# Leaving out or narrowing the third block of an expert's tokens, and packing the rest of the gating into fewer steps

## The chip, the cores and the metric

The kernel runs on one core of one Trainium2 chip. The metric is the device time of one execution in microseconds (us). Before the change the median of three runs is 567.98 us (566.25 to 568.43). The profile shows one further execution.

## The reference

Three layers follow each other. Their inputs are 4 batches of 576 positions with 8 heads of 64; the output of the first layer is read as 2304 tokens of 512 values.

```
attn = softmax(q k^T / 8 + bias(s), causal) v          # layer 1, x = [2304, 512]
expert = argmax(x @ w_gate)                            # layer 2: top-1 of 8 experts
x[t] = gate_w[t] * (relu(x[t] @ w1[e]) @ w2[e])        #   for the tokens t of expert e
logits = x @ phi                                       # layer 3: soft mixture, 32 slots
slot_in = softmax(logits, over tokens).T @ x
slot_out = relu(slot_in @ w1'[e]) @ w2'[e]             #   4 slots for each of 8 experts
out = softmax(logits, over slots) @ slot_out
```

## The kernel before

**Stages.** Attention runs from the start to about 215 us, the gating of the last batch to about 235 us, the eight experts of layer 2 from 239.6 to 503 us, and the slot experts and the output follow. An untaken branch (`overflow`, for experts with more tokens than planned) lies at 235 to 239 us.

**An expert.** The experts are sorted by their number of tokens. Place `e` has room for `WIDTH[e]` token columns, 352, 336, 320, 304, 304, 288, 256 and 256, at most CAP = 384, which is three blocks of 128. An expert is 16 steps in the order `STEPS`: eight h steps (12 matmuls into `h`, L1004, the hidden layer) and eight y steps (12 matmuls into `y`, L1004). A weight chunk is split for each step into a high part (`whi`, a cast on ACT, L893) and a low part (`wlo`, a subtraction on DVE, L895), two steps ahead, in three buffers. `hhi` (ACT, L1028) and `hlo` (DVE, L1029) are the same split of h.

**Gathering.** `gather(e)` (L911) fetches the tokens of an expert with three indirect DMAs that POOL issues, one for each block of 128, into `xg`; `xt_unit` (L998) turns them with 12 PE transposes into `xT`. The transposes for expert e+1 stand before the last two steps of expert e.

**The rest of the gating.** For the first expert's successors the gating is not finished when the first expert starts. `late_units` holds 13 pieces: `sort_a` (the sort of the experts, DVE), `g3`, five `gt` (`la` and `cbo`, L734 and L737, four on DVE and one on POOL), `sort_regs` (ACT and SP read the order into registers), `g4` (the PE matmuls `tb`, L745, and `idxu`, L746), `sort_b` (the gather's indices `sidxu`, L577 to L580), `pads` (L1215 to L1222), `close_att` (memory of the attention is given to the weight ring) and `gather(1)`. `merge` lays these evenly between the first expert's steps 1 to 13. Each engine runs its instructions in the order in which the program issues them.

**The post stage.** `post_units(e)` is merged between the steps of expert e+1; that of the last expert has no steps around it. `pl`: logits `lgp` (L1064), four products of 32 output rows each and 384 columns, one for each 128 values of a token, each in its own 32 columns of the PE array. `p1`: `ltp` (L1083), the logits by token, the running maximum over tokens. `py(t)`: `yTp` (L1073), the block's tokens turned back. `p2`, `p3`: the maximum `mt`, `mr`, `mb`, then the exponentials `Lm` and `al`. `p4`: `si` (L1116), for each block a product of 32 rows and 512 columns, and on DVE `SI = SI * ac + si` (L1120), a running sum of 96 rows, 32 for each block. `pc`, `pc2`: the softmax over slots `L`, which POOL scatters with one indirect DMA for each block into `c_d` (L1146). After the last post stage `sps` (L1262) reads all 96 rows of `SI`, and the slot experts (`hp`, `acc`) begin. In the last post stage PE runs matmuls on constants (`warm`, L245) after the pieces that the table `WARM` names by their place in the list.

Of the kernel before, what the change touches and what calls it, by code (L numbers as in the profile page):

```python
# [71 lines left out]
def kernel(ctx, tc, qk, vm, vt, s, wg, w1, w2, phi, m1, m2, m3, out, dbg=None):  # L72
# [830 lines left out]
            refill(i)  # L903

    def gather(e, idx, ov=False, early=False):
        for t in range(3):
            g = ytok[:, t, :] if ov else wpool[0].tile([128, DM], F32, tag="xg", name=f"xg{e}_{t}", bufs=3)
            if early:
                nc.gpsimd.memset(g, 0.0)
            rows = N - S if early else N + 1  # L910
            nc.gpsimd.indirect_dma_start(  # L911
                out=g, out_offset=None, in_=xg_d[0:rows],
                in_offset=bass.IndirectOffsetOnAxis(ap=idx[:, t:t + 1], axis=0),
                bounds_check=rows - 1, oob_is_err=False)
            xg_t[e, t] = g
# [70 lines left out]
    pmk = mp.tile([128, E, 3], F32, name="pmk")  # L986
    idxm = mp.tile([128, E, 3], U32, name="idxm")

    def xt_copy(k, tp):
        nc.scalar.copy(xT[:, 0, k, :], tp[:, 0:CAP])  # L990
        nc.vector.tensor_tensor(out=xT[:, 1, k, :], in0=tp[:, 0:CAP], in1=xT[:, 0, k, :].bitcast(F32),
                                op=ALU.subtract)

    def xt_unit(e, k):
        def f():
            tp = ps.tile([128, 512], F32, tag="tp", name=f"xTp{e}_{k}", bufs=2)
            for t in range(3):
                nc.tensor.transpose(tp[:, 128 * t:128 * t + 128], xg_t[e, t][:, 128 * k:128 * k + 128], ident)  # L998
            xt_copy(k, tp)
        return f  # L1000

    def product(w_, terms):
# [52 lines left out]

    def post_units(e, pad, idx, final=False):
        d = {}

        def pl():
            lg = ps.tile([128, CAP], F32, tag="tp", name=f"lgp{e}", bufs=2)
            for k in range(4):
                nc.tensor.matmul(lg[32 * k:32 * k + 32, :], lhsT=phi_sb[:, k, :], rhs=yT[:, k, :], start=True, stop=True,  # L1064
                                 skip_group_check=True)
            d["l4"] = ytok[:, 2, 0:CAP]
            (halves if final else nc.scalar.copy)(d["l4"], lg)

        def py(t):
            def f():  # L1070
                tp = ps.tile([128, 512], F32, tag=f"y{t}" if final else "tp", name=f"yTp{e}_{t}", bufs=1 if final else 2)
                for k in range(4):
                    nc.tensor.transpose(tp[:, 128 * k:128 * k + 128], yT[:, k, 128 * t:128 * t + 128], ident)  # L1073
                if t == 1 and not final:
                    nc.vector.tensor_copy(ytok[:, t, :], tp)
                else:
                    nc.scalar.copy(ytok[:, t, :], tp)
# [34 lines left out]
        def p4():
            al, Lm = d["al"], d["Lm"]
            si = ps.tile([128, DM], F32, tag="tp", name=f"si{e}", bufs=2)
            for t in range(3):
                nc.tensor.matmul(si[32 * t:32 * t + 32, :], lhsT=Lm[:, t, :], rhs=ytok[:, t, :], start=True, stop=True)  # L1116
            ac = mp.tile([128, 32], F32, tag="ac", name=f"ac{e}", bufs=1)
            nc.vector.transpose(ac, al)
            for x in (slice(0, 256), slice(256, 512)) if final else (slice(0, 512),):
                nc.vector.scalar_tensor_tensor(out=SI[:, x], in0=SI[:, x], scalar=ac[0:96, 0:1], in1=si[0:96, x],  # L1120
                                               op0=ALU.mult, op1=ALU.add)

        def p4b():
            al, Lm = d["al"], d["Lm"]
            nc.vector.tensor_tensor(out=esum, in0=esum, in1=al, op=ALU.mult)
            es = mp.tile([128, 32], F32, tag="es", name=f"es{e}", bufs=1)
            nc.vector.tensor_reduce(out=es, in_=Lm.rearrange("p t s -> p s t"), axis=AX.X, op=ALU.add)
            nc.vector.tensor_tensor(out=esum, in0=esum, in1=es, op=ALU.add)

        def pc():  # L1130
            L = mp.tile([128, 3, 32], F32, tag="L", name=f"L{e}", bufs=2)
            mx = mp.tile([128, 3], F32, tag="cmx", name=f"cmx{e}", bufs=1)
            nc.vector.tensor_reduce(out=mx, in_=d["Lm"], axis=AX.X, op=ALU.max)
            nc.vector.tensor_tensor(out=L, in0=d["Lm"], in1=mx.unsqueeze(2).to_broadcast([128, 3, 32]), op=ALU.subtract)
            nc.scalar.activation(out=L, in_=L, func=ACTF.Exp)
            d["L"] = L

        def pc2():
            L = d["L"]
            sm = mp.tile([128, 3], F32, tag="csm", name=f"csm{e}", bufs=1)  # L1140
# [3 lines left out]
            nc.vector.tensor_tensor(out=L, in0=L, in1=sm.unsqueeze(2).to_broadcast([128, 3, 32]), op=ALU.mult)  # L1144
# [12 lines left out]
    def overflow(over):  # L1157
        with tc.If(over > 0, label="over"):  # L1158
# [20 lines left out]
            for e in range(E):  # L1179
# [8 lines left out]
                with tc.For_i(0, times, 1):  # L1188
# [289 lines left out]
```

## Time and profile before

| what | value |
|---|---|
| median of three runs | 567.98 us |
| the profiled execution | 566.11 us |
| its span, first to last instruction | 564.4 us |
| PE busy | 537.0 us, 95% |
| DVE, ACT, POOL busy | 368.6, 300.6, 175.9 us |
| mean granted TensorE clock | 0.990 of full speed |
| on the chain that ended last | PE 52%, of it h and y of the experts 36% |

Times in the rows below are microseconds from the start of the span. Busy time is the share in which an engine has an instruction in flight; PE's matmuls overlap, so the time that a group of them costs is read from the distance of the starts, which the chain of waits gives as the group's piece.

### The profile page before, as it was taken

The numbers are of one execution on the slowest core, as the hardware profiler recorded it, in microseconds if no ns is written. First come the engines' busy times: TensorE is split into PE (matmuls) and PEld (weight loads), VectorE is DVE, ScalarE is ACT, GpSimd is POOL, SyncE is SP. The second block draws the span as 40 slices with busy tenths as digits, with TensorE's granted clock in tenths as the row PEclk, the third lists the DMA queues.
The fourth block names the chain that finished last, engine by engine and source line by source line (L and its number), as shares of the span: only waits on it lengthen the run. The fifth ranks groups of instructions, "written<-read, shape, count | busy, mean of one in ns | idle before, by whom it ended". The sixth has DMA issues, their size and how long they took to land.

```text
span 564.4 us, 11552 instructions
## 1 busy us (share of the span) xinstructions
PE 537.0 (95%) x4148; PEld 429.3 (76%) x4152; DVE 368.6 (65%) x1023; ACT 300.6 (53%) x782; POOL 175.9 (31%) x208
## 2 busy tenths in 40 slices
PE   8688899999999999899699999999999999999994
PEld 3466666766776666699699999999999898973464
DVE  6687779779887954476356666566766767653253
ACT  5477777687687765143343545445455555541122
POOL 6543236632843706012202204032220403025300
PEclk9899999999999999999899999999999999999998
DMA  4765662766487131201468768687874644479996
GB/s 120 247 227 150 203 220 82 210 224 202 127 249 230 48 129 63 92 2 28 175 214 302 279 237 293 244 327 281 296 273 162 201 158 153 150 253 339 396 351 186
DMA packets 40787, 114.60 MB, mean 203 GB/s; under 512 B 5775, under 2 KB 14289, under 8 KB 38800
## 3 DMA queue, kind: packets, MB, share of 16 engines
q1 hardware_dynamic: 27040, 68.81, 37.2%
q10 hardware_dynamic: 10560, 37.77, 18.8%
q0 software_dynamic: 3120, 7.19, 3.7%
q8 instruction: 35, 0.57, 0.4%
q14 instruction: 32, 0.26, 0.1%
HBM read 98.52 MB, written 11.16 MB: 194 GB/s over the span
## 4 chain that ended last, share of the span: by engine, by line
PE 52%; issue 3%; DMA 1%; DVE 0%; POOL 0%; ACT 0%; POOLq 0%
PE y L1004 18%; PE h L1004 18%; PE acc L1366 3%; PE hp L1327 3%; PE yTp L1073 2%; PE xTp L998 2%; PE si L1116 1%; PE op L1397 1%; PE lgp L1064 1%; DMA xg<-xg_d,sidxu 1%; PE ltp L1083 1%; PE cTp L1311 0%; PE mb L1102 0%; PE hTp L1343 0%; PE warm L245 0%
## 5 line engine op out<-in xcount | busy, mean ns | idle before, releaser
L1004 PE MATMUL h<-xT,whi 128*128 128x304 f32 (+5 forms) x512 | 110.4, 306 | 2.1 <-PEq L1158 2.1
L895 DVE TENSOR_TENSOR wlo<-chunk,whi 128x512 fp32r<-128x512 f32 x125 | 85.5, 688 | 31.7 <-ACT whi L893 31.0
L893 ACT CAST whi<-chunk 128x512 fp32r<-128x512 f32 x128 | 78.9, 620 | 27.4 <-PE y L1004 23.9
L1004 PEld LDWEIGHTS h<-xT,whi 128*128 128x128 f32 x512 | 83.0, 188 | 3.2 <-issue 2.6
L1004 PE MATMUL y<-hhi,whi 128*128 128x256 f32 (+5 forms) x256 | 81.5, 318 | 0.0
L1146 POOL DMA_INDIRECT c_d<-L,idxm x24 | 31.5, 1311 | 156.9 <-DVE L L1144 141.0
L491 ACT COPY aT<-tp 128x512 f32<-128x512 f32 (+3 forms) x128 | 55.5, 452 | 43.1 <-PE tp L484 31.3
L1004 PE MATMUL y<-hlo,whi 128*128 128x256 f32 (+5 forms) x256 | 77.4, 302 | 0.0
L1004 PE MATMUL y<-hhi,wlo 128*128 128x256 f32 (+5 forms) x256 | 77.3, 302 | 0.0
L1004 PE MATMUL h<-xT,wlo 128*128 128x256 f32 (+5 forms) x256 | 77.0, 301 | 0.0
L425 DVE CUSTOM_DVE_ANT_0 sa<-sc,mask 128x384 f32<-128x384 f32 (+3 forms) x128 | 60.5, 484 | 20.2 <-PE sc L422 17.9
L435 ACT ACTIVATE sa<-sa,mx 128x128 f32<-128x128 f32 (+3 forms) x128 | 71.2, 561 | 1.1 <-DVE mx L425 0.8
L1028 ACT ACTIVATE hhi<-h 128x304 fp32r<-128x304 f32 (+5 forms) x64 | 27.1, 423 | 68.1 <-PE h L1004 67.1
L538 PE MATMUL oTp<-aT,v 128*64 128x320 f32 (+4 forms) x448 | 59.4, 374 | 0.0
L1029 DVE SCALAR_TENSOR_TENSOR hlo<-h,hhi 128x304 fp32r<-128x304 f32 (+5 forms) x64 | 30.2, 472 | 42.6 <-ACT hhi L1028 42.2
L484 PE MATMUL tp<-ident,sa 128*128 128x128 f32 x320 | 53.4, 284 | 3.4 <-ACT sa L435 3.2
L1004 PEld LDWEIGHTS y<-hhi,whi 128*128 128x128 f32 x256 | 48.7, 190 | 10.4 <-issue 5.9
L422 PE MATMUL sc<-ks,qs 128*128 128x384 f32 (+3 forms) x128 | 50.1, 394 | 2.4 <-DVE mx L425 1.4
L484 PEld LDWEIGHTS tp<-ident,sa 128*128 128x128 f32 x320 | 35.0, 142 | 21.9 <-issue 11.2
L387 POOL TENSOR_TENSOR ks<-qk,ks 64x576 fp32r<-64x576 f32 x31 | 45.5, 1481 | 15.1 <-ACT ks L367 11.1
L1004 PEld LDWEIGHTS y<-hlo,whi 128*128 128x128 f32 x256 | 48.8, 191 | 0.0
L1004 PEld LDWEIGHTS y<-hhi,wlo 128*128 128x128 f32 x256 | 48.6, 190 | 0.0
(288 smaller groups left out, 958.1 us busy)
## 6 DMA issues: line engine op xcount, KB each, us to landing
chunk<-in_w_dram ACTq DMA_DIRECT2D x56, 512.0 KB, 5.5
chunk<-in_m_dram SPq DMA_DIRECT2D x45, 512.0 KB, 5.6
qk<-in_qk_dram SPq DMA_DIRECT2D x15, 1152.0 KB, 5.7
chunk<-in_m_dram ACTq DMA_DIRECT2D x16, 512.0 KB, 5.2
kb<-ks SPq DMA_DIRECT2D x15, 288.0 KB, 3.6
v<-in_vm_dram SPq DMA_DIRECT2D x16, 256.0 KB, 5.7
chunk<-in_w_dram SPq DMA_DIRECT2D x8, 512.0 KB, 6.5
xg_d<-xr SPq DMA_DIRECT2D x16, 256.0 KB, 3.6
```

The source lines that it names most:

```text
L387: eng.tensor_tensor(out=ks, in0=qk_t[p][64:128, 1, hh], in1=ks.bitcast(F32), op=ALU.subtract)
L422: nc.tensor.matmul(sc[:, :ext], lhsT=qs_t[p % 2][:, j, hh, 64 * hh + 128 * st:64 * hh + 128 * st + 128], rhs=ks[:, hh, :ext], start=(j == ...
L425: nc.vector.tensor_tensor_reduce(out=sa[:, o:o + ext], in0=sc[:, :ext], in1=mask[:, 512 - ext:512], scale=1.0, scalar=3.0e38, op0=ALU.add, ...
L435: nc.scalar.activation(out=x, in_=x, func=ACTF.Exp, bias=mx[:, st:st + 1], scale=-1.0, accum_out=rsum[:, b, st, 2 * k + hh:2 * k + hh + 1])
L484: nc.tensor.transpose(tp[:, 128 * c:128 * c + 128], src(hh, st, jt), ident)
L491: nc.scalar.copy(o, i)
L538: nc.tensor.matmul(o[c][64 * hh:64 * hh + 64, lo - 256 * c:hi - 256 * c], lhsT=v_t[p][:n, jt, hh, :], rhs=aT[:n, hh, jt, lo:hi], start=(jt ...
L893: nc.scalar.copy(hi, raw)
L895: eng.tensor_tensor(out=lo, in0=raw, in1=hi.bitcast(F32), op=ALU.subtract)
L1004: nc.tensor.matmul(out[:, :w_], lhsT=a, rhs=b[:, :w_], start=first, stop=last, skip_group_check=True)
L1029: nc.vector.scalar_tensor_tensor(out=lo[:, :w_], in0=h[:, :w_], scalar=0.0, in1=hi[:, :w_].bitcast(F32), op0=ALU.max, op1=ALU.subtract)
L1146: nc.gpsimd.indirect_dma_start(out=c_d[t], out_offset=bass.IndirectOffsetOnAxis(ap=idx[:, t:t + 1], axis=0), in_=L[:, t, :], in_offset=Non ...
```

## The change

Four things change.

1. `post_units` and `xt_unit` work on the columns that the expert has. With `w_ = WIDTH[e]` and `nt` blocks (three for places 0 to 5, two for places 6 and 7), `lgp` has `w_` columns for 384, and the third block's transposes, products, softmax columns, gather and scatter are left out for places 6 and 7.
2. For these two places the rows 64 to 95 of `SI` still have to be scaled: POOL does it with a new instruction, `SI[g:96] * ac`, in `p4`. DVE's `SI` keeps the first 64 rows.
3. The 13 late units are merged with the first expert's steps 1 to 8; steps 9 to 13 follow without any.
4. `py(2)` is no piece of the list for the last two places. `WARM` is unchanged, so its places 6 and 9 now mean `p3` (it was `pc`) and nothing (it was `p4`).

```
     def gather(e, idx, ov=False, early=False):
-        for t in range(3):
+        for t in range(3 if ov or early else -(-WIDTH[e] // 128)):
...
-            for t in range(3):
+            for t in range(-(-w // 128)):
                 nc.tensor.transpose(tp[:, 128 * t:128 * t + 128], xg_t[e, t][:, 128 * k:128 * k + 128], ident)
-            xt_copy(k, tp)
+            xt_copy(k, tp, w)
...
+        w_ = CAP if ov else WIDTH[e]
+        nt = -(-w_ // 128)
...
-                nc.tensor.matmul(lg[32 * k:32 * k + 32, :], lhsT=phi_sb[:, k, :], rhs=yT[:, k, :], start=True, stop=True,
+                nc.tensor.matmul(lg[32 * k:32 * k + 32, 0:w_], lhsT=phi_sb[:, k, :], rhs=yT[:, k, 0:w_], start=True, stop=True,
...
-            for t in range(3):
+            for t in range(nt):
                 nc.tensor.matmul(l[:, t, :], lhsT=d["l4"][:, 128 * t:128 * t + 128], rhs=repI, start=True, stop=True,
...
         def p4():
             al, Lm = d["al"], d["Lm"]
-            si = ps.tile([128, DM], F32, tag="tp", name=f"si{e}", bufs=2)
-            for t in range(3):
-                nc.tensor.matmul(si[32 * t:32 * t + 32, :], lhsT=Lm[:, t, :], rhs=ytok[:, t, :], start=True, stop=True)
             ac = mp.tile([128, 32], F32, tag="ac", name=f"ac{e}", bufs=1)
             nc.vector.transpose(ac, al)
+            si = ps.tile([128, DM], F32, tag="tp", name=f"si{e}", bufs=2)
+            for t in range(nt):
+                r = min(128, w_ - 128 * t)
+                nc.tensor.matmul(si[32 * t:32 * t + 32, :], lhsT=Lm[:r, t, :], rhs=ytok[:r, t, :], start=True, stop=True)
+            g = 32 * nt
+            if nt < 3:
+                nc.gpsimd.tensor_scalar(out=SI[g:96], in0=SI[g:96], scalar1=ac[g:96, 0:1], scalar2=None, op0=ALU.mult)
             for x in (slice(0, 256), slice(256, 512)) if final else (slice(0, 512),):
-                nc.vector.scalar_tensor_tensor(out=SI[:, x], in0=SI[:, x], scalar=ac[0:96, 0:1], in1=si[0:96, x],
+                nc.vector.scalar_tensor_tensor(out=SI[0:g, x], in0=SI[0:g, x], scalar=ac[0:g, 0:1], in1=si[0:g, x],
                                                op0=ALU.mult, op1=ALU.add)
...
-            for t in range(3):
+            for t in range(nt):
                 nc.gpsimd.indirect_dma_start(
                     out=c_d[t], out_offset=bass.IndirectOffsetOnAxis(ap=idx[:, t:t + 1], axis=0),
                     in_=L[:, t, :], in_offset=None, bounds_check=N - 1, oob_is_err=False)
+        third = [py(2)] if nt > 2 else []
         if final:
-            return [pl, p1, py(0), py(1), p2, py(2), pc, p3, pc2, p4, p4b]
-        return [pl, p1, py(0), p2, pc, py(1), p3, pc2, py(2), p4, p4b]
+            return [pl, p1, py(0), py(1), p2, *third, pc, p3, pc2, p4, p4b]
+        return [pl, p1, py(0), p2, pc, py(1), p3, pc2, *third, p4, p4b]
...
-            for u in merge(steps[1:14], (post if e else late_units + [lambda: gather(1, eidx(1))])):
+            k = 14 if e else 9
+            for u in merge(steps[1:k], (post if e else late_units + [lambda: gather(1, eidx(1))])) + steps[k:14]:
```

The places where this moves instructions, in the order in which each engine has them:

DVE, in the first expert, before: from the last `la` to the gather's indices `sidxu` (`hlo_5` belongs to the sixth h step).

```order
L734 TENSOR_SCALAR la_4_7345<-io_125,lane_7141 64x128
L737 TENSOR_SCALAR cbo_4_7347<-io_128,ch_7139,tid 64x144
L895 TENSOR_TENSOR wlo_7350<-chunk_2858,whi_7349 128x512
L1029 SCALAR_TENSOR_TENSOR hlo_5_7366<-h_7087,hhi_5_7365 128x352
L746 TENSOR_TENSOR idxu<-idxf,tb_7369 128x144
L895 TENSOR_TENSOR wlo_7377<-chunk_2044,whi_7376 128x512
L577 CAST tidx<-idxu 128x24
```

The same on DVE now (`hlo_3` belongs to the fourth h step):

```order
L1031 SCALAR_TENSOR_TENSOR hlo_3_7290<-h_7096,hhi_3_7289 128x352
L734 TENSOR_SCALAR la_4_7293<-io_125,lane_7121 64x128
L737 TENSOR_SCALAR cbo_4_7295<-io_128,ch_7119,tid 64x144
L746 TENSOR_TENSOR idxu<-idxf,tb_7297 128x144
L895 TENSOR_TENSOR wlo_7305<-chunk_1357,whi_7304 128x512
L577 CAST tidx<-idxu 128x24
```

The indices stood behind the sixth h step's `hlo_5` and stand now behind the fourth's `hlo_3`; between `cbo_4` and `idxu` there was a whole step, and now there is nothing.

POOL, at the end of the last expert's post stage, before: its three scatters and what follows (names in brackets are semaphores; DMASW are those of POOL's own DMAs).

```order
L1146 DMA c_d_62<-L_10576,idxm 2304x32 [waits DMASW5_49,DMASW0_49,DVE_49]
L1146 DMA c_d_63<-L_10576,idxm 2304x32 [waits DMASW6_49,DMASW1_49]
L1146 DMA c_d_64<-L_10576,idxm 2304x32 [waits DMASW7_49]
L1284 MEMSET hz_10646 128x1024 [waits DMAHW3_49,PE_49,DMAHW6_49,Activation_49,Pool_49]
L1290 DMA c_10648<-c_d_62 128x192 [waits DMAHW4_49,DMASW0_49,DMAHW7_49,PE_49,Activation_49]
```

The same on POOL now:

```order
L1157 DMA c_d_62<-L_10543,idxm 2304x32 [waits DVE_49,Pool_49]
L1157 DMA c_d_63<-L_10543,idxm 2304x32
L1129 TENSOR_SCALAR SI<-SI,ac_10570 32x512 [waits DMASW6_49,DMASW5_49,DVE_49]
L1297 MEMSET hz_10607 128x1024 [waits DMAHW3_49,PE_49,DMAHW6_49,Activation_49,Pool_49]
L1303 DMA c_10609<-c_d_62 128x192 [waits DMAHW4_49,DMAHW7_49,PE_49,Activation_49]
```

Two scatters are left, and the new multiplication of `SI` stands behind them; it waits for the semaphores that these two scatters raise when they land (the first raises DMASW5, the second DMASW6).

PE, at the same place, before: from the maximum to the first product of `sps`.

```order
L1094 MATMUL mt_10563<-ident,m_10547 1x128 [waits DVE_49]
L245 MATMUL warm_10568<-const-bfloat16-1.0 128x512 [waits PE_49]
L1073 MATMUL yTp_2_10570<-ident,yy 128x128 x4
L245 MATMUL warm_10581<-const-bfloat16-1.0 128x512 [waits PE_49]
L1102 MATMUL mb_10584<-mr_10565,ones 128x32 [waits DVE_49]
L1116 MATMUL si_10606<-yy,Lm_10544 32x512 [waits Activation_49]
L245 MATMUL warm_10614<-const-bfloat16-1.0 128x512 [waits PE_49]
L1262 MATMUL sps_10618<-repI,SI 128x32 [waits DVE_49]
```

The same on PE now:

```order
L1101 MATMUL mt_10536<-ident,m_10520 1x128 [waits DVE_49]
L245 MATMUL warm_10541<-const-bfloat16-1.0 128x512 [waits PE_49]
L1109 MATMUL mb_10548<-mr_10538,ones 128x32 [waits DVE_49]
L245 MATMUL warm_10556<-const-bfloat16-1.0 128x512 [waits PE_49]
L1126 MATMUL si_10572<-yy,Lm_10517 32x512 [waits Activation_49]
L1275 MATMUL sps_10579<-repI,SI 128x32 [waits DVE_49,Pool_49]
```

`mb` no longer stands behind the third block's transposes and a pair of `warm` matmuls, no `warm` stands between `si` and `sps` any more, and `sps` waits for POOL as well as for DVE.

## Rows read from the trace of the kernel before

**Rows 1.** Windows: length, busy (count) PE, PEld, DVE, ACT, POOL, PEclk, DMA share, GB/s

```profile
270.00:280.00 10.00, 7.08 (x37) 6.88 (x38) 3.61 (x7) 3.82 (x9) 1.71 (x2) 0.83 0.29 106
280.00:500.00 220.00, 220.00 (x1635) 205.45 (x1634) 146.48 (x343) 112.32 (x243) 47.44 (x38) 1.00 0.68 236
```

**Rows 2.** Waits of PE, 200 to 300 us: total, times, longest

```profile
PE xTp L998 <- DMA xg<-xg_d,sidxu: 4.4, 2, 2.4
```

**Rows 3.** Chain of waits around the second expert: start, length, what

```profile
266.86 6.35 DMA xg<-xg_d,sidxu
...
273.25 1.11 PE xTp L998 x4
274.37 2.92 PE y L1004 x12
...
277.94 1.94 PE y L1004 x12
...
283.55 0.78 PE lgp L1064 x8
...
286.37 0.59 PE ltp L1083 x6
...
288.88 0.44 PE yTp L1073 x4
```

**Rows 4.** The same chain, 285 to 455 us

```profile
305.60 0.99 PE si L1116 x6
```

**Rows 5.** Instructions of PE in order: start, length, what

```profile
258.91 1.58 PE L745 MATMUL tb<-cbo,la 128*128 128x144 f32 x10
```

**Rows 6.** Instructions of DVE in the first expert, in order

```profile
251.89 0.53 DVE L1029 SCALAR_TENSOR_TENSOR hlo<-h,hhi 128x352 fp32r<-128x352 f32 x1 [0.44 <-ACT hhi L1028]
...
256.87 0.27 DVE L734 TENSOR_SCALAR la<-io,lane 64x128 f32<-64x128 f32 x1
257.06 0.34 DVE L737 TENSOR_SCALAR cbo<-io,ch,tid 64x144 f32<-64x144 f32 x1
...
260.53 0.30 DVE L746 TENSOR_TENSOR idxu<-idxf,tb 128x144 uint32<-128x144 f32 x1 [0.40 <-PE tb L745]
...
263.15 0.18 DVE L580 CAST sidxu<-sidx 128x24 uint32<-128x24 f32 x1
```

**Rows 7.** Instructions of POOL in the first expert, in order

```profile
264.13 1.11 POOL L911 DMA_INDIRECT xg<-xg_d,sidxu  x1 [13.57 <-issue]
```

**Rows 8.** Instructions of all engines, end of the last post stage

```profile
507.58 0.28 DVE L1096 TENSOR_REDUCE mr<-mt 1x32 f32<-1x128 f32 x1 [0.37 <-PE mt L1094]
507.70 0.60 PE L1073 MATMUL yTp<-ident,yy 128*128 128x128 f32 x4
...
508.67 0.40 PE L1102 MATMUL mb<-mr,ones 1*128 1x32 f32 x2
...
510.29 0.26 DVE L1144 TENSOR_TENSOR L<-L,csm 128x96 f32<-128x96 f32 x1
...
510.82 0.98 POOL L1146 DMA_INDIRECT c_d<-L,idxm  x1 [11.04 <-DVE ac L1118]
...
511.38 1.09 PE L1262 MATMUL sps<-repI,SI 96*128 96x32 f32 x8
...
512.11 0.98 POOL L1146 DMA_INDIRECT c_d<-L,idxm  x1 [0.30 <-PE sps L1262]
```

**Rows 9.** DMAs issued from 495 to 520 us: what, queue, count, median us to landing

```profile
c_d<-L,idxm POOLq DMA_INDIRECT x6, 4.1
```

**Rows 10.** Line L1146, all 24 scatters of the run

```profile
DMA to landing us min/median/max: 3.2/4.7/6.6
```

**Rows 11.** Groups of POOL: out<-in, shape, count, busy us, mean ns

```profile
L737 POOL TENSOR_SCALAR cbo<-io,ch,tid 128x144 f32<-128x144 f32 x13 | 12.6, 968 | 0.0
L734 POOL TENSOR_SCALAR la<-io,lane 128x128 f32<-128x128 f32 x13 | 8.3, 640 | 22.6 <-DVE lane L711 22.4
...
L895 POOL TENSOR_TENSOR wlo<-chunk,whi 128x512 fp32r<-128x512 f32 x3 | 3.7, 1266 | 0.0
```

More of the change, by code (lines that the diff above doesn't have):

```diff
@@ L987, with xt_copy, xt_unit @@
     idxm = mp.tile([128, E, 3], U32, name="idxm")
-    def xt_copy(k, tp):
-        nc.scalar.copy(xT[:, 0, k, :], tp[:, 0:CAP])
-        nc.vector.tensor_tensor(out=xT[:, 1, k, :], in0=tp[:, 0:CAP], in1=xT[:, 0, k, :].bitcast(F32),
+    def xt_copy(k, tp, w):
+        nc.scalar.copy(xT[:, 0, k, 0:w], tp[:, 0:w])
+        nc.vector.tensor_tensor(out=xT[:, 1, k, 0:w], in0=tp[:, 0:w], in1=xT[:, 0, k, 0:w].bitcast(F32),
                                 op=ALU.subtract)
-    def xt_unit(e, k):
+    def xt_unit(e, k, ov=False):
+        w = CAP if ov else WIDTH[e]
         def f():
             tp = ps.tile([128, 512], F32, tag="tp", name=f"xTp{e}_{k}", bufs=2)
-            for t in range(3):
+            for t in range(-(-w // 128)):
                 nc.tensor.transpose(tp[:, 128 * t:128 * t + 128], xg_t[e, t][:, 128 * k:128 * k + 128], ident)
-            xt_copy(k, tp)
+            xt_copy(k, tp, w)
         return f
@@ L1054, in step_unit, with post_units @@
         return f
-    def post_units(e, pad, idx, final=False):
+    def post_units(e, pad, idx, final=False, ov=False):
         d = {}
+        w_ = CAP if ov else WIDTH[e]
+        nt = -(-w_ // 128)
         def pl():
@@ L1063, in pl @@
             for k in range(4):
-                nc.tensor.matmul(lg[32 * k:32 * k + 32, :], lhsT=phi_sb[:, k, :], rhs=yT[:, k, :], start=True, stop=True,
+                nc.tensor.matmul(lg[32 * k:32 * k + 32, 0:w_], lhsT=phi_sb[:, k, :], rhs=yT[:, k, 0:w_], start=True, stop=True,
                                  skip_group_check=True)
             d["l4"] = ytok[:, 2, 0:CAP]
-            (halves if final else nc.scalar.copy)(d["l4"], lg)
+            (halves if final else nc.scalar.copy)(d["l4"][:, 0:w_], lg[:, 0:w_])
         def py(t):
@@ L1071, in f @@
                 tp = ps.tile([128, 512], F32, tag=f"y{t}" if final else "tp", name=f"yTp{e}_{t}", bufs=1 if final else 2)
+                r = min(128, w_ - 128 * t)
                 for k in range(4):
-                    nc.tensor.transpose(tp[:, 128 * k:128 * k + 128], yT[:, k, 128 * t:128 * t + 128], ident)
+                    nc.tensor.transpose(tp[:r, 128 * k:128 * k + 128], yT[:, k, 128 * t:128 * t + r], ident)
                 if t == 1 and not final:
-                    nc.vector.tensor_copy(ytok[:, t, :], tp)
+                    nc.vector.tensor_copy(ytok[:r, t, :], tp[:r])
                 else:
-                    nc.scalar.copy(ytok[:, t, :], tp)
+                    nc.scalar.copy(ytok[:r, t, :], tp[:r])
             return f
@@ L1085, in p1 @@
             Lm = mp.tile([128, 3, 32], F32, tag="Lm", name=f"Lm{e}", bufs=1)
-            nc.vector.tensor_tensor(out=Lm, in0=l, in1=pad.unsqueeze(2).to_broadcast([128, 3, 32]), op=ALU.add)
-            nc.vector.transpose(LT[:, 0:96], Lm.rearrange("p t s -> p (t s)"))
+            Lm = Lm[:, 0:nt]
+            nc.vector.tensor_tensor(out=Lm, in0=l[:, 0:nt], in1=pad[:, 0:nt].unsqueeze(2).to_broadcast([128, nt, 32]), op=ALU.add)
+            nc.vector.transpose(LT[:, 0:32 * nt], Lm.rearrange("p t s -> p (t s)"))
             m4 = mp.tile([128, 1], F32, tag="m4", name=f"m4{e}", bufs=1)
@@ L1103, in p3 @@
             Lm = d["Lm"]
-            nc.vector.tensor_tensor(out=Lm, in0=Lm, in1=mb.unsqueeze(1).to_broadcast([128, 3, 32]), op=ALU.subtract)
+            nc.vector.tensor_tensor(out=Lm, in0=Lm, in1=mb.unsqueeze(1).to_broadcast([128, nt, 32]), op=ALU.subtract)
             nc.scalar.activation(out=Lm, in_=Lm, func=ACTF.Exp)
@@ L1113, in p4 @@
             al, Lm = d["al"], d["Lm"]
-            si = ps.tile([128, DM], F32, tag="tp", name=f"si{e}", bufs=2)
-            for t in range(3):
-                nc.tensor.matmul(si[32 * t:32 * t + 32, :], lhsT=Lm[:, t, :], rhs=ytok[:, t, :], start=True, stop=True)
             ac = mp.tile([128, 32], F32, tag="ac", name=f"ac{e}", bufs=1)
             nc.vector.transpose(ac, al)
+            si = ps.tile([128, DM], F32, tag="tp", name=f"si{e}", bufs=2)
+            for t in range(nt):
+                r = min(128, w_ - 128 * t)
+                nc.tensor.matmul(si[32 * t:32 * t + 32, :], lhsT=Lm[:r, t, :], rhs=ytok[:r, t, :], start=True, stop=True)
+            g = 32 * nt
+            if nt < 3:
+                nc.gpsimd.tensor_scalar(out=SI[g:96], in0=SI[g:96], scalar1=ac[g:96, 0:1], scalar2=None, op0=ALU.mult)
             for x in (slice(0, 256), slice(256, 512)) if final else (slice(0, 512),):
-                nc.vector.scalar_tensor_tensor(out=SI[:, x], in0=SI[:, x], scalar=ac[0:96, 0:1], in1=si[0:96, x],
+                nc.vector.scalar_tensor_tensor(out=SI[0:g, x], in0=SI[0:g, x], scalar=ac[0:g, 0:1], in1=si[0:g, x],
                                                op0=ALU.mult, op1=ALU.add)
@@ L1130, in pc @@
         def pc():
-            L = mp.tile([128, 3, 32], F32, tag="L", name=f"L{e}", bufs=2)
-            mx = mp.tile([128, 3], F32, tag="cmx", name=f"cmx{e}", bufs=1)
+            L = mp.tile([128, 3, 32], F32, tag="L", name=f"L{e}", bufs=2)[:, 0:nt]
+            mx = mp.tile([128, 3], F32, tag="cmx", name=f"cmx{e}", bufs=1)[:, 0:nt]
             nc.vector.tensor_reduce(out=mx, in_=d["Lm"], axis=AX.X, op=ALU.max)
-            nc.vector.tensor_tensor(out=L, in0=d["Lm"], in1=mx.unsqueeze(2).to_broadcast([128, 3, 32]), op=ALU.subtract)
+            nc.vector.tensor_tensor(out=L, in0=d["Lm"], in1=mx.unsqueeze(2).to_broadcast([128, nt, 32]), op=ALU.subtract)
             nc.scalar.activation(out=L, in_=L, func=ACTF.Exp)
@@ L1139, in pc2 @@
             L = d["L"]
-            sm = mp.tile([128, 3], F32, tag="csm", name=f"csm{e}", bufs=1)
+            sm = mp.tile([128, 3], F32, tag="csm", name=f"csm{e}", bufs=1)[:, 0:nt]
             nc.vector.tensor_reduce(out=sm, in_=L, axis=AX.X, op=ALU.add)
@@ L1143, in pc2 @@
             nc.vector.reciprocal(sm, sm)
-            nc.vector.tensor_tensor(out=L, in0=L, in1=sm.unsqueeze(2).to_broadcast([128, 3, 32]), op=ALU.mult)
-            for t in range(3):
+            nc.vector.tensor_tensor(out=L, in0=L, in1=sm.unsqueeze(2).to_broadcast([128, nt, 32]), op=ALU.mult)
+            for t in range(nt):
                 nc.gpsimd.indirect_dma_start(
@@ L1192, in overflow @@
                     for k in range(4):
-                        xt_unit(e, k)()
+                        xt_unit(e, k, True)()
                     for n in range(16):
@@ L1197, in overflow @@
                     nc.vector.tensor_scalar(out=opad, in0=opad, scalar1=float(N), scalar2=-BIG, op0=ALU.is_ge, op1=ALU.mult)
-                    for u in post_units(e, opad, ia):
+                    for u in post_units(e, opad, ia, ov=True):
                         u()
@@ L1201, in overflow @@
             for k in range(4):
-                xt_unit(0, k)()
+                xt_unit(0, k, True)()
             place.clear()
@@ L1208 @@
         y_t.clear()
-        nc.gpsimd.memset(yT[:, :, WIDTH[0]:CAP], 0.0)
+        nc.gpsimd.memset(ytok[:, 2, WIDTH[0]:CAP], 0.0)
         pace[0] = 8
```

## The prediction

> **What bounds the kernel now.** I read the windows first, then PE's waits, then the chain of waits, then each engine's instructions where the change touches them. From 280 to 500 us PE is busy in all of the window of 220 us, at full granted clock, while DVE and ACT have idle time [rows 1]. So in the experts what PE doesn't do any more comes off the time, and work saved on DVE, ACT or POOL does not. Before that there is one hole: in the window 270 to 280 PE is busy 7.08 of 10 us and its granted clock averages 0.83 [rows 1]. It is the wait for the second expert's tokens, 4.4 us in two pieces [rows 2]: the last of the three gathers is issued at 266.86 and landed 6.35 us later, and PE goes on at 273.25 [rows 3]. At the other end, the last post stage is a chain over PE, DVE, ACT and POOL with no expert's steps beside it, so there waits count in full.
>
> **The hole at 268 us.** Besides its 4.4 us it costs clock. The four transposes at 273.25 take 1.11 us where four such take 0.44 elsewhere, and the twelve y matmuls after them 2.92 where the next twelve take 1.94 [rows 3]: 0.67 + 0.98 = 1.65 us, at the lower of the clock's two levels (1.2 for 2.4 GHz). Together 6.05 us.
>
> Does the change close it? Packed into eight steps, `tb` goes from behind the sixth h step to behind the fourth, that is four steps of some 1.93 us (twelve matmuls in 1.94 [rows 3]) before 258.91 [rows 5], 251.2 on this trace's clock. Its last operands `la_4` and `cbo_4` now stand on DVE behind `hlo_3`, which starts at 251.89 and lasts 0.53; with `la` and `cbo`, 0.55 (0.27 and 0.34, overlapping a little) [rows 6], they are there at 252.9. PE can do eight of the ten rows of `tb` meanwhile (1.58 us for ten [rows 5]), so `tb` ends at about 253.2 instead of 252.8: a new stall of 0.4 us; I take 0.5. From `idxu` to the end of `sidxu` DVE took 260.53 to 263.33, a `wlo` among it, 2.8 us [rows 6]; started at 253.25 it ends at 256.05, 7.3 us earlier. POOL issued the first gather 0.8 us after `sidxu` [rows 6, 7] and the last 2.73 after the first, which landed 6.35 later [rows 3]: now 256.85, 259.6, 265.9. PE had come to the tokens at about 268.2 (273.25 less the wait and the two transposes between its pieces) and now comes at 268.7. The hole closes with 2.8 us to spare. The other late pieces lie on DVE beside PE's steps, where DVE still waits for ACT (0.44 us ahead of `hlo_3` [rows 6]); if they come too thick, a late `wlo` or `hlo` stops PE. `sort_regs` and `close_att` move with it, so the second expert's weights are requested earlier, which can only help. Gain 6.05 - 0.5 = 5.5 us; bounds 0 (the tokens late all the same) and 6.05.
>
> **PE in the other experts' steps.** `lgp`: eight rows cost 0.78 us for 384 columns [rows 3]; places 0 to 6 lose 32, 48, 64, 80, 80, 96 and 128 columns, 528 in all, 1.375 times 384. In proportion that is 1.07, at nothing per column 0; some of the 0.78 is latency, I take 0.9. `xTp`: 8 transposes fewer for places 6 and 7 at 0.11 (0.44 for four [rows 3]): 0.88. Places 0 to 5 keep theirs (128 columns move, whatever the rows). `yTp` of place 6: 0.44. `ltp` of place 6: two of six rows, 0.59/3 = 0.2 [rows 3]. `si` of place 6: six rows in 0.99 us [rows 4], one product of three gone. The three write different rows and stand in different columns of the array; between 0 (they run beside each other) and 0.33, I take 0.1, since six rows that end so close together overlap. Sum 2.5 us, bounds 1.5 and 2.9. Narrower work on DVE and ACT and the two gathers fewer are worth nothing: PE is the bound.
>
> **The last post stage.** Before, `mb` (508.67) stood behind four transposes (507.70) and two constant matmuls, though `mr` was done at 507.86 [rows 8]. Without them it waits for `mr` alone, 0.8 us earlier; narrower `lgp` and `ltp` ahead of it give some 0.35 more. So the softmax `L`, ready at 510.55, is ready at 509.4, and the first scatter leaves at 509.67, not 510.82 [rows 8]. On DVE and PE alone `sps` would start 1.15 us earlier.
>
> But `sps` now needs POOL's multiplication too, and that stands behind two scatters and waits until both have landed. Second scatter: 1.29 us after the first (510.82 to 512.11 [rows 8]), 510.96. Landing: the six nearest in time took 4.1 us in the median [rows 9], all 24 from 3.2 to 6.6 [rows 10]; 4.1 gives 515.1. The multiplication, 32 rows of 512 columns with a scalar for each row, is not in the trace. From below: POOL's tensor_tensor on as many columns, 1.27 us; from above: `cbo`, two operations, 0.97 for 144 columns, in proportion 3.4. `la`, one operation with such a scalar like this one, takes 0.64 for 128 columns, in proportion 2.56, but part of a short instruction is fixed [rows 11]; I take 1.8, a little under the middle of 1.27 and 2.56. It ends at 516.9 and `sps` starts at 517.0, not 511.38 [rows 8]: 5.6 us later; bounds from 3.2 + 1.27 (515.5, 4.1 later) to 6.6 + 3.4 (521.0, 9.6 later). PE, with no constant matmuls left in this gap, stands idle for at least those 5.6 us, longer than in the hole at 268, and starts again at the lower clock: I take the same price, 1.6 us; bounds 0 and twice that. The same multiplication for place 6 has the whole last expert to hide in; the slot experts after `sps` are PE's and move as a whole.
>
> The Trainium skill, page "DMA: Bandwidth & Descriptors", section "Anatomy of one DMA — SWDGE (gpsimd) path", gives a DMA that POOL issues about 2.0 us plus its bytes at 436 GB/s, and puts most of it on the receipt of the write. By that a scatter of 16 KB would land in an estimated 2.04 us, the term would be 3.5 instead of 5.6, and the sum 2.1 us lower; the rows, 3.2 at the least of 24 [rows 10], counted from the start of the instruction, stand against it.
>
> **The sum.** -5.5 - 2.5 + 5.6 + 1.6 = -0.8 us. From the profiled execution's 566.11 that is 565.3; it lies 1.9 under the median of the runs shown, so on their scale 567.98 - 0.8 = 567.2 us. What is won in the experts is handed back before `sps`. A measurement of this kernel can tell some 0.5% (2.8 us) from no change, so this is "no change", with 565.2 to 569.5 as its own range (one of the terms off by its usual half).
>
> **Rivals.**
> - *The wait in the last post stage is short* (27%). The scatters land in 3.2 us, the multiplication runs as fast as a tensor_tensor, and the clock does not fall: `sps` 4.1 us later, -5.5 - 2.5 + 4.1 = -3.9, 564.1 us. For it: those are real rows of this trace. Against it: all three at their lower ends, and a clock that fell in a shorter hole at 268. By the page of the Trainium skill above alone, with the other terms as forecast, the sum would be -2.9; its chance is in this one.
> - *The wait is long* (13%), the case on the slower side. The scatters compete with the weights' stream, land in up to 6.6 us, and the multiplication costs as much for each column as `cbo`: `sps` 9.6 later; -5.5 - 2.5 + 9.6 + 1.6 = +3.2, with twice the clock's price +4.8: 571.2 to 572.8. It decides from the point where the multiplication ends after 517.8 on this trace's clock (then the sum is above 0), and tells beyond 0.5% after 520.6. For it: one of the 24 did take 6.6 [rows 10]. Against it: the six nearest, 4.1 in the median [rows 9].
> - *The hole stays* (7%). The packed gating starves a split or the tokens come late all the same, so the first term is 0 or 0.5 lost: -2.5 + 5.6 + 1.6 + 0.5 = +5.2, 573.2 us. Against it: 2.8 us to spare.
> - The forecast has 53%.
>
> **From these to the numbers.** Faster by over 0.5% (below 565.1): nine tenths of the short wait and a tenth of the forecast, 0.30. Slower by over 0.5% (above 570.8): the hole that stays, four fifths of the long wait, a little of the forecast, 0.19. Within 0.5%: 0.51. The range for 8 in 10 goes from 563.6 to 571.0: it takes in most of the short wait and the lower edge of the long one.
>
> **What would show it.** In the profile after: no wait of PE for `xg` before the second expert and a window there at full clock (else the first term is wrong); `lgp` in 0.65 to 0.75 us in the first places and some 0.55 at place 6; about 2.5 us less from the second expert's first step to the last y step. In the last post stage a stretch of 7 us in which PE does nothing, ended by POOL, with the multiplication between 1.3 and 3 us, and the first `hp` matmuls at the lower clock. The prediction is wrong if `sps` starts less than 4 us or more than 9 us after `si`'s sum on DVE, or if PE waits inside the first expert's steps for more than a microsecond.

## The result: 4.2 us slower

The changed kernel takes 572.1 us (median of four runs, 570.78 to 572.30) against 567.9 us before: ratio 1.0074, 95% interval 1.0048 to 1.0100. The forecast was 567.2 us, with a range of 563.6 to 571.0; the time lies above it.

The profiled execution after takes 570.78 us with a span of 568.8 us, 4.4 us over the span before. PE is busy for 539.3 us (537.0 before). First the windows after, with the columns of [rows 1]:

```profile
250.00:260.00 10.00, 9.42 (x60) 9.06 (x59) 7.18 (x24) 3.22 (x7) 2.12 (x3) 1.00 0.08 21
260.00:270.00 10.00, 10.00 (x66) 9.98 (x65) 4.71 (x8) 4.01 (x10) 0.99 (x1) 1.00 0.85 286
270.00:280.00 10.00, 10.00 (x70) 9.20 (x69) 6.52 (x14) 5.98 (x14) 3.44 (x3) 1.00 0.74 273
280.00:500.00 220.00, 220.00 (x1614) 202.96 (x1613) 142.93 (x340) 108.17 (x240) 39.75 (x34) 1.00 0.65 222
500.00:565.00 65.00, 53.95 (x643) 29.78 (x644) 20.33 (x66) 11.76 (x26) 13.94 (x20) 0.92 0.80 290
```

The hole is gone: from 270 to 280 PE is busy throughout at full clock, where it had 7.08 us at 0.83 [rows 1]. The waits of PE from 200 to 520 us name what is left, in total, times and the longest:

```profile
PE sps L1275 <- POOL SI L1129: 7.8, 1, 7.8
PE h L1006 <- DVEq L1170: 1.7, 1, 1.7
PE tb L745 <- DVE cbo L737: 0.6, 1, 0.6
PE tp L511 <- ACT aT L491: 0.4, 1, 0.4
```

No wait for `xg` stands among them [rows 2]; `tb` has the small new stall; and the last post stage has a wait of 7.8 us for POOL. The wait of `h` stands ahead of the first expert, where the kernel before has one of 2.1 us, and the last line belongs to the attention. These views fit the forecast. But the time from the first `h` to the `lgp` of the last post stage fell from 263.72 us (239.57 to 503.29) to 259.44 (239.76 to 499.20): 4.3 us, where 8.0 were forecast. No wait shows the missing 3.7, since a busy PE has none. They came out when the distance between starts was added up for each kind of PE's work in that stretch, before and after: all kinds were equal or shorter, but for `tb` (0.66 longer) and `si` (6.92 us at seven places before, 10.78 after).

Two `si` of the trace after, places 1 and 2, in PE's order, each with the instruction behind it:

```profile
334.51 1.06 PE L1126 MATMUL si<-yy,Lm 128*32 128x512 f32 x6
335.50 0.41 PE L1006 MATMUL y<-hhi,whi 128*128 128x320 f32 x1
...
367.58 2.02 PE L1126 MATMUL si<-yy,Lm 128*32 128x512 f32 x6
369.54 0.41 PE L1006 MATMUL y<-hhi,whi 128*128 128x304 f32 x1
```

The second, with 64 rows in its third product (rows are those that it sums over, the tokens of the block), holds PE for 1.96 us (367.58 to 369.54); the first, with 80 rows, for 0.99 (334.51 to 335.50), as all did before [rows 4]. Places 2, 3, 4 and 5, with 64, 48, 48 and 32 rows, take 1.95 to 1.96 each; places 0 and 1, with 96 and 80, take 0.99. The weight loads at place 2 show how:

```profile
367.58 0.14 PEld L1126 LDWEIGHTS si<-yy,Lm 128*32 128x32 f32 x4 [0.17 <-issue]
368.56 0.13 PEld L1126 LDWEIGHTS si<-yy,Lm 64*32 64x32 f32 x2 [0.84 <-ACT hhi L1030]
```

The two products over 128 rows load their weights together; the third loads its own only 0.98 us later, when they are through. The releaser in the bracket is the profile's inference; experiment 5 shows that it isn't the cause, since there the load comes at once with ACT's work unchanged.

The last post stage after, cut from the timeline of all engines [rows 8]:

```profile
499.20 1.37 PE L1068 MATMUL lgp<-yy,phi_sb 128*32 128x256 f32 x8
...
503.30 0.40 PE L1109 MATMUL mb<-mr,ones 1*128 1x32 f32 x2
...
504.36 1.05 PE L1126 MATMUL si<-yy,Lm 128*32 128x512 f32 x4
504.90 0.22 DVE L1155 TENSOR_TENSOR L<-L,csm 128x64 f32<-128x64 f32 x1
...
505.46 0.86 DVE L1131 SCALAR_TENSOR_TENSOR SI<-SI,ac,si 64x256 f32<-64x256 f32 x2 [0.21 <-PE si L1126]
505.89 1.02 POOL L1157 DMA_INDIRECT c_d<-L,idxm  x1 [6.76 <-DVE ac L1122]
507.21 0.98 POOL L1157 DMA_INDIRECT c_d<-L,idxm  x1 [0.30 <-issue]
511.61 1.57 POOL L1129 TENSOR_SCALAR SI<-SI,ac 32x512 f32<-32x512 f32 x1 [3.41 <-DMA c_d<-L,idxm]
513.23 1.91 PE L1275 MATMUL sps<-repI,SI 96*128 96x32 f32 x8 [7.82 <-POOL SI L1129]
```

`L` is ready 5.92 us after `lgp` starts (7.26 before), the second scatter lands 4.4 us after its start, the multiplication takes 1.57, and `sps` starts 14.03 us after `lgp` where it was 8.09. Then the clock. PE from `sps` on, first before (where `sps` starts at 511.38 [rows 8]), then after; start, length, what:

```profile
512.39 7.07 PE L1327 MATMUL hp<-chunk,sT 128*32 128x512 f32 x64
519.40 0.66 PE L1343 MATMUL hTp<-ident,hs 128*128 128x128 f32 x4
```

```profile
513.23 1.91 PE L1275 MATMUL sps<-repI,SI 96*128 96x32 f32 x8 [7.82 <-POOL SI L1129]
515.07 9.46 PE L1340 MATMUL hp<-chunk,sT 128*32 128x512 f32 x64
524.46 0.66 PE L1356 MATMUL hTp<-ident,hs 128*128 128x128 f32 x4
```

From `sps` to `hTp` it is 8.02 us before and 11.23 after: 3.21 more. The windows after show the granted clock there. It is 0.50 (1.2 GHz) in the first 4.8 us and 1.00 (2.4 GHz) from 521 on; the 0.68 of the 3 us between is a mean of these two levels, 1.9 us at the lower and 1.1 at the higher, so PE works at the lower one for 6.7 us:

```profile
513.20:518.00 4.80, 4.77 (x24) 2.57 (x28) 1.10 (x6) 0.00 (x0) 0.00 (x0) 0.50 0.02 2
518.00:521.00 3.00, 3.00 (x24) 0.71 (x20) 0.00 (x0) 0.00 (x0) 2.08 (x4) 0.68 0.92 322
521.00:524.40 3.40, 3.40 (x36) 0.77 (x28) 0.00 (x0) 0.60 (x1) 3.40 (x8) 1.00 0.86 267
```

The whole difference, from starts in the two traces: 0.2 (first `h` later) - 4.3 (first `h` to `lgp`) + 5.9 (`lgp` to `sps`) + 3.2 (`sps` to `hTp`) - 0.7 (`hTp` to the end, 45.0 us before and 44.3 after) = 4.3 us; the spans differ by 4.4. No run is aimed at the first and the last of these terms.

### The profile page after: what moved, and what is told of

It reads as the page before. It is cut to its first block, busy times and chain, and to the rows that moved or that the text cites. A ratio compares the mean times of both kernels' runs of the same rounds, so it can differ in the third digit from the quotient of the medians.

```text
span 568.8 us, 11495 instructions
## 1 busy us (share of the span) xinstructions
PE 539.3 (95%) x4122; PEld 426.9 (75%) x4126; DVE 367.8 (65%) x1023; ACT 296.9 (52%) x780; POOL 169.9 (30%) x206
## 5 line engine op out<-in xcount | busy, mean ns | idle before, releaser
L1157 POOL DMA_INDIRECT c_d<-L,idxm x22 | 25.5, 1159 | 158.0 <-DVE L L1155 147.0
L422 PE MATMUL sc<-ks,qs 128*128 128x384 f32 (+3 forms) x128 | 51.4, 403 | 2.3 <-DVE mx L425 2.0
L422 PE MATMUL sc<-kb,qs 128*128 128x384 f32 (+3 forms) x128 | 42.0, 328 | 7.4 <-DMA kb<-trs 3.3
```

Source lines behind the costliest of these rows:

```text
L422: nc.tensor.matmul(sc[:, :ext], lhsT=qs_t[p % 2][:, j, hh, 64 * hh + 128 * st:64 * hh + 128 * st + 128], rhs=ks[:, hh, :ext], start=(j == ...
```

## Experiments

The kernels of the first four experiments ran side by side on one chip, with 17 runs of the kernel before (median 567.75 us, 566.16 to 571.23); those of the last four on one chip, with 23 runs of it (568.49, 565.58 to 571.24). Ratios are to the kernel before. The changed kernel did not run beside them: "under the changed kernel" is against its 572.1 us of the result. Since the time of the kernel before varies by more than 5 us, the rows decide on single microseconds, not the medians.

**1. The third product on 96 rows.**

```diff
-                r = min(128, w_ - 128 * t)
+                r = max(96, min(128, w_ - 128 * t))
                 nc.tensor.matmul(si[32 * t:32 * t + 32, :], lhsT=Lm[:r, t, :], rhs=ytok[:r, t, :], start=True, stop=True)
```

> The changed kernel, with the third product of si (places 2 to 5, whose third blocks have 64, 48, 48 and 32 rows) run on 96 rows, as at place 0; rows above the block carry weight 0, so nothing else changes. Theory A: a product over 64 rows or fewer does not run beside the two products over 128 rows ahead of it; si then takes 1.95 us in place of 0.99 at four places. On 96 rows it should take 0.99 everywhere, PE should reach the last post stage 3.9 us earlier than in the changed kernel, and the time should fall by 3.9 us, to about 568.2. Rival B: the longer si comes from its operands (the third transposes narrowed, copies that end later), not from the rows of the product: si stays at 1.95 and the time at 572.

Measured: 568.3 us, ratio 1.0000 (0.9981 to 1.0019). `si` takes 0.99 us at all places, 6.92 in sum; from the first `h` to `lgp` it is 255.59 us, 3.85 less than in the changed kernel. Theory A holds: less work in the product had cost 3.85 us.

**2. The multiplication on DVE in the last post stage.**

```diff
-                nc.gpsimd.tensor_scalar(out=SI[g:96], in0=SI[g:96], scalar1=ac[g:96, 0:1], scalar2=None, op0=ALU.mult)
+                (nc.vector if final else nc.gpsimd).tensor_scalar(out=SI[g:96], in0=SI[g:96], scalar1=ac[g:96, 0:1], scalar2=None, op0=ALU.mult)
```

> The changed kernel, with the multiplication of SI's rows 64 to 95 in the last post stage on DVE instead of POOL, so that it stands behind no scatter. Theory A: sps waited only for that multiplication (7.8 us), and the lower clock after the idle time costs 0.9 us in sps and 2.4 us in hp: sps starts some 7 us after the lgp of that stage instead of 14, hp takes 7.0 us instead of 9.4, and the time falls by 6.8 + 0.9 + 2.4 = 10 us, to about 562, less up to 0.5 us for the multiplication on DVE. Rival B: the landing of the scatters is needed anyway by what comes after (the loads of c on POOL), so that most of the wait moves to the products behind hp: a fall of 4 us or less.

Measured: 560.82 us, ratio 0.9867 (0.9834 to 0.9901), 11.3 us under the changed kernel; its span is 10.0 us shorter. DVE's and PE's rows of that stage:

```profile
499.34 1.37 PE L1068 MATMUL lgp<-yy,phi_sb 128*32 128x256 f32 x8
...
505.42 0.48 DVE L1129 TENSOR_SCALAR SI<-SI,ac 32x512 f32<-32x512 f32 x1
...
506.46 1.09 PE L1275 MATMUL sps<-repI,SI 96*128 96x32 f32 x8 [0.91 <-DVE SI L1131]
```

`sps` stands 7.12 us behind `lgp`, less than the 8.09 before the change, and `sps` to `hTp` is back at 8.02. Theory A holds, B falls: nothing behind `hp` needed the scatters earlier (`hTp` to the end takes 44.3 us in both traces).

**3. Both edits.**

> The two edits together (third product on 96 rows, multiplication on DVE in the last post stage). If the two are independent their gains add up: 3.9 + 10 = 13.9 us below the changed kernel, about 558, 10 us below the kernel before. If they share a cause or one opens another wait: 562 to 566.

Measured: 559.13 us, ratio 0.9839 (0.9807 to 0.9871), 13.0 us under the changed kernel. From the first `h` to `lgp` it is 255.59 us as in experiment 1, from `lgp` to `sps` 7.12 as in experiment 2: the gains add up. What is missing lies ahead of both, the first `h` at 242.04 us where it is at 239.89 in the trace of experiment 2; experiment 8 looks at that again.

**4. The packing alone.** The kernel before, with the late pieces in steps 1 to 8:

```diff
-            for u in merge(steps[1:14], (post if e else late_units + [lambda: gather(1, eidx(1))])):
+            k = 14 if e else 9
+            for u in merge(steps[1:k], (post if e else late_units + [lambda: gather(1, eidx(1))])) + steps[k:14]:
```

> The kernel before, with the packing of the gating's rest into the first eight steps alone (no block left out or narrowed). By the terms of the prediction: the hole at 268 us closes for 6.05 us, a new stall at tb costs 0.5 to 0.7; the time falls by 5.4 us to about 562.5, and no wait for xg is left. Rival: the tokens come in time only with the narrower third blocks as well, so that part of the hole stays: a fall of 0 to 3 us.

Measured: 560.32 us, ratio 0.9875 (0.9838 to 0.9912). No wait for `xg` is left, and PE is busy throughout in the window of the hole:

```profile
270.00:280.00 10.00, 10.00 (x70) 9.15 (x69) 6.84 (x13) 6.16 (x14) 3.51 (x3) 1.00 0.83 294
```

From the first `h` to `lgp` it is 258.05 us, 5.67 less than before; the prediction had 5.5. The medians differ by 7.4, but the profiled run of before lies 1.6 under its own median, and the interval of the ratio, 5.0 to 9.2 us, holds the 5.67. This change alone makes the kernel faster; all four together make it slower.

**5. Where the boundary lies.** As experiment 1, with `max(65, ...)`.

> The changed kernel, with the third product of si at places 2 to 5 on 65 rows (instead of 64, 48, 48 and 32; in the run before, on 96). Theory A, that the boundary is 64 rows, half the array: 65 rows are enough, si takes 0.99 us at every place and the time is that of the run with 96 rows, 568.3. Rival B, that the cost falls with the rows that are filled: si lies between 0.99 and 1.95, about 1.5 with 65 rows, and the time is about 570.

Measured: 566.62 us (ten runs, 565.75 to 573.19), ratio 0.9983 (0.9954 to 1.0012). Place 2 again, and its weight loads, all six together now:

```profile
368.73 1.06 PE L1126 MATMUL si<-yy,Lm 128*32 128x512 f32 x6
```

```profile
368.73 0.15 PEld L1126 LDWEIGHTS si<-yy,Lm 128*32 128x32 f32 x6 [0.17 <-issue]
```

0.99 us at every place. With 64 rows it was 1.96, so one row more makes the product run beside the others. The median is 1.7 us under the expected 568.3, but the interval of its ratio holds that of experiment 1 (1.0000), and the rows are as expected. Theory A holds; B, a cost by filled rows, falls.

**6. PE kept busy while it waits.** Constant matmuls between `si` and `sps`:

```diff
-WARM = {0: 3, 3: 1, 4: 1, 6: 2, 9: 2}
+WARM = {0: 3, 3: 1, 4: 1, 6: 2, 8: 34}
```

> The changed kernel, with 34 constant matmuls put on PE between si and sps of the last post stage (34 times 0.213 us are 7.2 us), so that PE is busy while it waits for POOL's multiplication; nothing else changes. If the lower clock after the idle time is what lengthens sps from 1.0 to 1.9 us and hp from 7.0 to 9.4, both go back, and the time falls by 3.2 us, to 569. If hp is longer for another reason (its weights, the transfers on POOL beside it), nothing changes: 572. If the constant matmuls end after the multiplication, sps starts up to 0.5 us later.

Measured: 568.58 us, ratio 1.0004 (0.9983 to 1.0024), 3.5 us under the changed kernel. PE there:

```profile
506.15 7.61 PE L245 MATMUL warm<-const-bfloat16-1.0 128*128 128x512 bf16 x34
514.25 1.08 PE L1275 MATMUL sps<-repI,SI 96*128 96x32 f32 x8 [0.49 <-POOL SI L1129]
515.25 7.07 PE L1340 MATMUL hp<-chunk,sT 128*32 128x512 f32 x64
522.26 0.66 PE L1356 MATMUL hTp<-ident,hs 128*128 128x128 f32 x4
```

From `sps` to `hTp` it is 8.01 us instead of 11.23, with the multiplication as late as ever, and the granted clock there is 1.00:

```profile
514.00:522.00 8.00, 7.75 (x72) 2.94 (x72) 1.10 (x6) 0.60 (x1) 4.81 (x9) 1.00 0.58 205
```

So the 3.2 us belong to the clock. That the median falls by 3.5 us agrees, but the trace's span is only 2.2 us under the changed kernel's, since its first `h` starts 0.8 us later and `sps` stands 0.2 later behind `lgp`.

**7. The multiplication ahead of the scatters, still on POOL** (and gone from `p4`).

```diff
         def pc2():
             L = d["L"]
+            ac = mp.tile([128, 32], F32, tag="ac", name=f"ac{e}", bufs=1)
+            nc.vector.transpose(ac, d["al"])
+            d["ac"] = ac
+            if nt < 3:
+                g = 32 * nt
+                nc.gpsimd.tensor_scalar(out=SI[g:96], in0=SI[g:96], scalar1=ac[g:96, 0:1], scalar2=None, op0=ALU.mult)
             sm = mp.tile([128, 3], F32, tag="csm", name=f"csm{e}", bufs=1)[:, 0:nt]
```

> The changed kernel, with ac computed ahead of the softmax for c and POOL's multiplication put ahead of the two scatters instead of behind them; it stays on POOL. If its price is the order on POOL (the two scatters and the landing of the second), the multiplication starts within 0.5 us of ac and takes 1.6 us, sps starts about 8 us after the lgp of that stage (14 in the changed kernel, 7.1 with the multiplication on DVE), and the time is 561 to 562.5. If POOL waits for something else that comes late (ac, or the transfers of c), sps stays at 11 us or more behind lgp and the time above 565.

Measured: 562.39 us, ratio 0.9881 (0.9847 to 0.9916). In the trace:

```profile
502.10 1.37 PE L1068 MATMUL lgp<-yy,phi_sb 128*32 128x256 f32 x8
...
507.74 1.56 POOL L1153 TENSOR_SCALAR SI<-SI,ac 32x512 f32<-32x512 f32 x1 [9.21 <-DVE csm L1155]
...
509.35 1.08 PE L1278 MATMUL sps<-repI,SI 96*128 96x32 f32 x8 [1.05 <-POOL SI L1153]
```

`sps` stands 7.25 us behind `lgp` instead of 14.03, 0.13 later than with the multiplication on DVE. On POOL the same 1.56 us cost almost nothing once they stand ahead of the scatters: the price was the place in POOL's order. This trace's span is still 2.9 us longer than that of experiment 2, for reasons ahead of the edit: the first `h` starts 1.2 us later (241.10), and the first step's twelve matmuls take 1.5 us more, at a granted clock of 0.56 from there to 244.90.

**8. Both edits, the multiplication on ACT.** As experiment 3, with `nc.scalar.activation(out=SI[g:96], in_=SI[g:96], func=ACTF.Copy, scale=ac[g:96, 0:1])` in the last post stage.

> The two edits together, with the multiplication of the last post stage on ACT instead of DVE, so that it runs beside DVE's sums. DVE took 0.48 us for it ahead of the sums: sps should start 0.3 to 0.5 us earlier, 6.7 us after lgp. The run with both edits reached the first expert 2.1 us later than the others (242.0 instead of 239.9), ahead of anything that the edits touch. If that was chance of that build or run, this kernel is at 556.5 to 557; if the edits cause it, at 558.7.

Measured: 557.0 us (555.89 to 558.96), ratio 0.9805 (0.9777 to 0.9834), the fastest of all: 15 us under the changed kernel and 11.5 under the kernel before.

```profile
495.51 1.37 PE L1068 MATMUL lgp<-yy,phi_sb 128*32 128x256 f32 x8
...
501.59 0.71 ACT L1130 ACTIVATE SI<-SI,ac 32x512 f32<-32x512 f32 x1 [0.86 <-DVE ac L1122]
...
502.38 1.05 PE L1278 MATMUL sps<-repI,SI 96*128 96x32 f32 x8 [0.67 <-ACT SI L1130]
```

`sps` stands 6.87 us behind `lgp`, 0.25 earlier than with DVE. ACT needs 0.71 us, and `sps` still waits for it. The first `h` is at 239.90, so the late start of experiment 3 does not come with the edit on `si`, nor with taking the multiplication off POOL. Over the ten traces the first `h` starts between 239.57 and 242.04. In the traces of experiments 3 and 7, whose edits differ, PE is 1.1 us behind the changed kernel's trace by 62 us, far ahead of the experts, and the granted clock is 0.91 from 40 to 60 us, where it is 1.00 in those of experiment 8 and of the changed kernel. What caused the late start, and the rest of its 2.1 us, stays open.

## Why the prediction was wrong

Each term of its sum against the traces:

| term | forecast | measured |
|---|---|---|
| the hole closed, with the stall at `tb` | -5.5 | -5.67 (experiment 4) |
| less of PE's work in the experts, `si` of place 6 among it | -2.5 | -2.46 |
| `si` of places 2 to 5 | none | +3.85 (experiment 1) |
| `sps` later behind `lgp` | +5.6 | +5.94 |
| the clock after the wait | +1.6 | +3.21 |
| sum | -0.8 | +4.87 |

The -2.46 are the 255.59 us of experiment 1 less the 258.05 of experiment 4. By the distances between starts, `lgp` gives 0.88 of it (forecast 0.9), `xTp` 0.87 (0.88), `yTp` 0.36 (0.44) and `ltp` 0.22 (0.2); `h` and `y`, which were not in the forecast, give the rest. From the sum to the 4.4 us of the spans it is the 0.2 at the start and the 0.7 at the end told above.

- **The step that failed is the one on `si`.** The prediction priced it for place 6 alone ("one product of three gone ... I take 0.1") and did not price that at places 0 to 5 the third product now has fewer rows. At places 2 to 5 that costs 0.96 to 0.97 us each, 3.85 in all. Experiment 1 shows that the rows alone do it, experiment 5 that the step lies between 64 and 65. The kernel before ran the three products in the time of one: 0.99 us [rows 4], where the third alone takes 0.98 at place 2 (368.56 to 369.54). Place 6 shows the same (two in 0.98 us), so the 0.1 for it was 0.01. The change took the third out of that company.
  The Trainium skill has a rule that bears on this edit, and the prediction passed it by: the page "TensorEngine Tiling (Array Packing)", section "Key Properties", says that changing the tiling mode, unlike changing the tile, drains TensorE. Its section "Available Configurations" lists tiles of 128, of 64 and of 32 rows as separate groups of configurations. The weight load that comes 0.98 us late, and the step between 64 and 65 rows, agree with that, if a product over at most 64 rows runs in one of the smaller tiles; no row says in which it runs.
  Whether it is a drain or another reason for which the small product can't run beside the large ones, no run here tells apart. But a row of the kernel before speaks for the former. In `tb` products over 128 and over 64 rows follow each other, each in all 128 columns, so that none runs beside another. Three loads of weights (PEld), each behind the product that runs when it starts:

```profile
258.75 0.32 PE L1004 MATMUL h<-xT,wlo 128*128 128x352 f32 x1
258.75 0.19 PEld L745 LDWEIGHTS tb<-cbo,la 128*128 128x128 f32 x1
...
259.76 0.29 PE L745 MATMUL tb<-cbo,la 128*128 128x144 f32 x1
259.98 0.18 PEld L745 LDWEIGHTS tb<-cbo,la 64*128 64x128 f32 x1
...
260.21 0.28 PE L745 MATMUL tb<-cbo,la 64*128 64x144 f32 x1
260.42 0.19 PEld L1004 LDWEIGHTS y<-hhi,whi 128*128 128x128 f32 x1
```

  From 128 rows to 128 the weights load as the product ahead starts; from 128 to 64, and from 64 back, they load 0.21 to 0.22 us later. This favours the drain and does not show it.
- **The clock's price was half of what it is.** The prediction took the 1.6 us of the hole at 268 us, with 3.2 as its upper bound; measured are 3.2, and 2.7 and 3.0 in the traces of experiments 1 and 5, where `sps` waits about as long (10.71 and 11.03 us from `sps` to `hTp`). PE stood idle for 7.8 us there, not for 4.4 in two pieces, and worked at the lower level for 6.7 us afterwards; at 268 us the 0.83 of the window [rows 1] leaves 3.4 us at that level. Why it stayed there longer is not shown. With this term right and nothing else altered, the forecast's sum would be +0.8, still no change. It took this error and that on `si` together to leave the range: 572.1 us less 3.85 for `si` is 568.3, less 1.6 for the clock 570.5, and both lie inside it.
- **The wait was right in place and nearly in size.** Second scatter 0.3 us later than forecast, since the first left 0.77 us after `L` where it was 0.27 (no run explains that); landing 4.4 us against 4.1; multiplication 1.57 against 1.8. On the clock of the trace before it ends at 517.27, where 516.9 was forecast. The rival "the wait is long", whose times of 571.2 to 572.8 hold the measured one, is not what happened: it asked for an end after 517.8, and the wait was not that long.
- **The hole closed as described.** `tb` waits 0.58 us (0.5 was taken), `sidxu` ends at 256.47 (forecast 256.05), the last gather is issued at 259.99 (forecast 259.6), and no row of PE waits for `xg`. The other rivals, the short wait and the hole that stays, fell.
- **The rivals all sat where something waits.** The largest cost that was not forecast was in none of them: it is time in which PE is busy. Nor was it in the conditions under which the prediction called itself wrong: PE waits 0.6 us at most inside the first expert's steps, and `sps` starts 6.9 us after `si`'s sum on DVE (its end, 506.32). Only the sign "about 2.5 us less" in the experts showed it: against the packing alone (258.05 us, experiment 4), the changed kernel's 259.44 are 1.4 us more.

## What to carry to other kernels

A product that runs beside others in the array can lose that place when it gets smaller: before cutting rows, look whether its weights still load together with its neighbours', and whether rows of zeros up to the old size are cheaper (here 65 rows in 0.99 us against 64 in 1.96). Work put on an idle engine can cost its place in that engine's order rather than its length: here 1.57 us of POOL cost 10 us behind two scatters (6.9 of waiting, 3.2 of clock) and almost nothing ahead of them. And where an engine is busy on both sides, compare the distances between starts for each kind of its work, not its waits.

## What the runs showed that was not expected

- `si`, three products into different columns: 0.99 us with 65, 80, 96 or 128 rows in the third, 1.95 to 1.96 with 64, 48 or 32 (the other two have 128).
- The multiplication of 32 rows by 512 columns by a scalar for each row: 1.56 to 1.59 us on POOL, 0.71 on ACT, 0.48 on DVE.
- After 7.8 us without a matmul PE worked at a granted clock of 0.50 for 6.7 us, which cost 3.2 us; 34 constant matmuls in that gap kept it at 1.00 and gave the 3.2 us back.
